# Linear attention, MLP mixer and routed experts on one core: earlier narrowing, second matrices split in order of use, later scalings, a conditional end

## The chip, the core and the metric

The kernel runs on one core of one Trainium2 chip. The metric is the device time of one execution in microseconds (us), from a few runs of the same program; the median is given. Engines are called as the profile's rows call them: PE is TensorE's matmul, PEld its weight load, DVE VectorE, ACT ScalarE, POOL GpSimd, SP SyncE (here only the owner of most DMA queues). A name such as `SPq` is that engine's sequencer or DMA queue.

## The reference

Three stages follow one another on 4 batches of 576 tokens and 512 features. Here the weights of the MLP stage come in as float64, and the kernel narrows them to float32 itself.

```python
# 1: linear attention, 8 heads of 64
proj = q_or_k @ w_phi                                  # 64 -> 128
proj = proj - max(abs(proj), axis=-1)
phi  = concatenate([exp(proj), exp(-proj)], axis=-1)
kv   = einsum('bhsf,bhsd->bhfd', phi_k, v);  z = sum(phi_k, axis=2)
x    = (phi_q @ kv) / (phi_q @ z + 1e-06)
...
# 2: token mixing of rank 32, then a channel MLP 512 -> 2048 -> 512
u = x + (xt @ U @ V).transpose(0, 2, 1)
x = u + maximum(u @ w_ch1, 0.0) @ w_ch2
...
# 3: one expert of 8 for each token (512 -> 1024 -> 512)
fresh_e = argmax(logits[b, s])
e = fresh_e if s == 0 or local_gate[b, s] < 0.5 else prev_e
out[b, s] = p[e] * (maximum(x[b, s] @ w1[e], 0.0) @ w2[e])
```

## The kernel before

**Products.** A matrix product of the two MLP stages is three matmuls in the format that the rows call fp32r: high half by high half, high by low, low by high. So every weight piece (128x512) and every input of a second product exists twice. The high half of a weight is a cast on ACT (L370), its low half a subtraction on DVE (L364); the high half `hhi` of a hidden tile is a relu on ACT (L1106), the low half `hlo` one fused instruction on DVE (L1092). First products are recorded at L1127 to L1129, second ones (`mm2`) at L1249 to L1251. `mm2` goes over four hidden tiles in the order f = 2, 3, 0, 1 and uses the second matrix V2, V3, V0, V1 in that order. Some units save products by sums of submatrices; these sums are DVE instructions recorded at L1090 and L364.

**Narrowing.** Weights of the MLP stage arrive as float64 and are narrowed to float32 by `narrow`: one Abs on ACT (L93) and six instructions on DVE (L97, L100, L102, L104, L107, L111). Raw words sit in two buffers only, `raw0_92` and `raw1_93`. SP refills one (L322) once L107 of the block that used it has read it. During attention the threads `w_first` and `w_park` narrow the 16 pieces of the first two weight units; a narrowed piece is parked in HBM (L403). Attention is a loop of steps `S_`; a step calls `advance("w")` RATE = 2 times in `prepare` and, for each item of MLP work that `ffn_ahead` puts in beside attention from step 24 on, BESIDE = 3 times more if S_ > 21. Each call emits one instruction or a few of the narrowing. Nothing reorders them afterwards: an engine runs its instructions in the order in which the Python code emitted them.

**Banks.** During attention, tiles named `psf`, `tq`, `num`, `tps` and `utps` take turns in the three PSUM banks of the pool `ps_f`: the fourth tile waits until the first has been read out. A `psf` of a first product is read by `hhi` and then `hlo`. `utps` (token mixing, L925) multiplies by `ts`, whose low half is a DVE subtraction (L911).

**MoE.** Eight units, batch b = 0 to 3 and halves g = 0, 1, with 288 columns to a tile. The result of a batch is multiplied by the tokens' probabilities (`scaled`, L1276) and stored (L1285). Such a scaling is due two items after its product; in the last item it follows at once, and its store goes out on SP.

**The end.** Tokens whose expert is none of the two that a batch is served by are handled in a loop over a count `nl`, loaded at L1533 by every engine after all other work. Here the count is 0.

Of the kernel before, what the change touches and what calls it, by code (L numbers as in the profile page):

```python
# [28 lines left out]
NROW = 8  # L29
FT1 = 16  # L30
FT2 = 8
RATE, BESIDE = 2,3
MB = (1,2,3,)

LOCAL_T = -1.5 * 2.0 ** -23
# [6 lines left out]
def model(ctx, tc, kq, vx, wphi, ident, up, vp, wff, wg, wmoe1, wmoe2, rconst, outT):  # L42
    nc = tc.nc
# [10 lines left out]
    ps_f = ctx.enter_context(tc.tile_pool(name="ps_f", bufs=3, space=PSUM))  # L54
# [8 lines left out]
    y = const.tile([128, 4, B * S], F32, name="y")  # L63
# [97 lines left out]
    late = {}  # L161
# [6 lines left out]
    threads = []  # L168
# [11 lines left out]
    def cost(eng, n):  # L180
        return {"DVE": 0.085 + n / 960, "ACT": 0.17 + n / 1330, "POOL": 0.05 + n / 340}[eng]
# [101 lines left out]
    waiting = []  # L283
# [19 lines left out]
        return free_.pop(0)  # L303

    BLOCKS = ("A11", "A12", "A21", "A22")
    VS = ("V0", "V1", "V2", "V3")
    PLAIN = ("A11", "A12", "A21", "A22") + VS
    SEVEN = ("A21", "A11", "A22", "A12") + VS
    order = [(u, n) for u in ffn_units for n in (SEVEN if u.g else PLAIN)]
    wd = dram.tile([2, 8, 128, 512], F32, name="wd")  # L310
    raws = []

    def raw_dma():

# [919 lines left out]
    def mm2(i, t, d):  # L1234
# [296 lines left out]
    nl = nc.values_load(late["left"][0:1, 0:1], min_val=0, max_val=28)  # L1533
    l_p = ctx.enter_context(tc.tile_pool(name="lp", bufs=1))
    with tc.For_i(0, nl):
        f8 = l_p.tile([1, 8], F32, name="l_f8")
        ix = l_p.tile([1, 8], U32, name="l_ix")
        pf = l_p.tile([1, 1], F32, name="l_pf")
        po = l_p.tile([1, 32], F32, name="l_po")
        be = l_p.tile([1, 2], F32, name="l_be")  # L1540
        bi = l_p.tile([1, 3], I32, name="l_bi")
        tmp = l_p.tile([1, 16], F32, name="l_tmp")
        nc.vector.max(out=f8, in_=flags)
        nc.vector.max_index(out=ix, in_max=f8, in_values=flags)
        nc.vector.tensor_copy(out=pf, in_=ix[:, 0:1])
        nc.vector.tensor_scalar(out=po, in0=iota32[0:1], scalar1=pf, scalar2=None, op0=ALU.is_equal)
        nc.vector.tensor_tensor(out=flags, in0=flags, in1=po, op=ALU.subtract)

        nc.vector.tensor_tensor(out=tmp, in0=po[:, 0:16], in1=po[:, 16:32], op=ALU.add)
        nc.vector.tensor_tensor(out=tmp[:, 0:8], in0=tmp[:, 0:8], in1=tmp[:, 8:16], op=ALU.add)  # L1550
        nc.vector.tensor_tensor(out=tmp[:, 0:8], in0=tmp[:, 0:8], in1=iota8[0:1], op=ALU.mult)
        nc.vector.tensor_reduce(out=be[:, 1:2], in_=tmp[:, 0:8], axis=AX, op=ALU.add)
        nc.vector.tensor_tensor(out=be[:, 0:1], in0=pf, in1=be[:, 1:2], op=ALU.subtract)
        nc.vector.tensor_scalar(out=be[:, 0:1], in0=be[:, 0:1], scalar1=0.125, scalar2=None, op0=ALU.mult)

        nc.vector.tensor_copy(out=bi[:, 0:2], in_=be)
        nc.vector.tensor_copy(out=bi[:, 2:3], in_=pf)
        ev = nc.sync.value_load(bi[0:1, 1:2], min_val=0, max_val=NE - 1)
        bs = nc.sync.value_load(bi[0:1, 0:1], min_val=0, max_val=B - 1)
        rs = nc.sync.value_load(bi[0:1, 2:3], min_val=0, max_val=8 * B - 1)  # L1560
        bv = nc.vector.value_load(bi[0:1, 0:1], min_val=0, max_val=B - 1)
        ls = l_p.tile([128, S], F32, name="l_s")
        nc.sync.dma_start(out=ls, in_=late["sall"][bass.ds(rs, 1)].partition_broadcast(128))
        yb = l_p.tile([128, 4, S], F32, name="l_y")
        ob = l_p.tile([128, 4, S], F32, name="l_o")

        nc.sync.dma_start(out=yb, in_=late["ys"][:, :, bass.ds(bs * S, S)])
        nc.vector.memset(ob, 0.0)

        with tc.For_i(0, FT2) as j:  # L1570
            w1, w2 = (l_p.tile([128, 512], F32, name=f"l_w{m}") for m in range(2))
            nc.sync.dma_start(out=w1.rearrange("p (k c) -> p k c", k=2), in_=wmoe1[bass.ds(ev, 1), bass.ds(j, 1)].rearrange("o i k p c -> p (o i k) c"))
            nc.sync.dma_start(out=w2, in_=wmoe2[bass.ds(ev, 1), bass.ds(j, 1)].rearrange("o i p f -> (o i p) f"))
            for c in range(2):
                sl = slice(c * CH, (c + 1) * CH)
                ps = late["psg"].tile([128, CF], F32, tag="f", name="l_ps")[:, :CH]
                for k in range(4):
                    nc.tensor.matmul(ps, lhsT=w1[:, k * 128:(k + 1) * 128], rhs=yb[:, k, sl], start=(k == 0), stop=(k == 3))
                ht = l_p.tile([128, CH], F32, tag="l_h", bufs=2, name="l_h")
                nc.scalar.activation(out=ht, in_=ps, func=ACTF.Relu)  # L1580
                for d in range(4):
                    ps = ps_f.tile([128, CF], F32, tag="f", name="l_acc")[:, :CH]
                    nc.tensor.matmul(ps, lhsT=w2[:, d * 128:(d + 1) * 128], rhs=ht, start=True, stop=True)
                    nc.vector.tensor_tensor(out=ob[:, d, sl], in0=ps, in1=ob[:, d, sl], op=ALU.add)
        nc.vector.tensor_tensor(out=ob, in0=ob, in1=ls.unsqueeze(1).to_broadcast([128, 4, S]), op=ALU.mult)
        dst = y[:, :, bass.ds(bv * S, S)]
        nc.vector.tensor_tensor(out=ob, in0=ob, in1=dst, op=ALU.add)
        nc.vector.tensor_copy(out=dst, in_=ob)
        nc.sync.dma_start(out=outT.rearrange("(k p) t -> p k t", p=128)[:, :, bass.ds(bs * S, S)], in_=ob)
# [78 lines left out]
```

## Time and profile before

| what | value |
|---|---|
| device time, median of 3 runs | 768.52 us |
| the three runs | 767.36, 768.52, 770.09 us |
| device time of the profiled execution | 767.14 us |
| span in its profile, first to last instruction | 765.3 us |
| PE busy | 749.4 us, 98% of the span |
| DVE busy | 614.4 us, 80% |
| ACT busy | 339.0 us, 44% |
| POOL busy | 72.6 us, 9% |
| mean granted TensorE clock | 0.998 of full speed |

The profile is of one execution, and every duration below is from it. The table's share of busy time says which engine is nearest its limit over the whole span; where that engine stands still is seen only by stretches and by waits. The device time holds 1.8 us that lie outside the span.

### The profile page before, as it was taken

What the parts mean: (1) busy time and instruction counts of PE and PEld (TensorE: products, weight loads), DVE (VectorE), ACT (ScalarE), POOL (GpSimd) and SP (SyncE); (2) the same over time, 40 slices, a digit from 0 to 9 for tenths busy, and PEclk for the clock granted to TensorE, in tenths of its full rate; (3) what the DMA queues carried; (4) which work ended last, traced back from release to release, by engine and by line L of the source; (5) the groups of instructions that cost most, each with busy time, mean ns of one, the idle gap of its engine ahead of it and who ended that gap; (6) DMA issues with size and microseconds to landing.
All of it is one profiled execution on the core that took longest, in us unless ns stands there. A gap on an engine that the chain in (4) does not pass through costs nothing.

```text
span 765.3 us, 18800 instructions
## 1 busy us (share of the span) xinstructions
PE 749.4 (98%) x7680; PEld 728.7 (95%) x7680; DVE 614.4 (80%) x1241; ACT 339.0 (44%) x751; POOL 72.6 (9%) x116
## 2 busy tenths in 40 slices
PE   8999999999999999999999999999999999999996
PEld 6899898999899999999999999999999999999996
DVE  7889999887867989896899455256768899999974
ACT  5677767674242533323332222023454457365450
POOL 0212422112200000100101001000000000000000
PEclk9999999999999999999999999999999999999999
DMA  6444746325589687930659007442362143432501
GB/s 204 156 135 152 251 150 215 95 107 207 182 290 375 200 323 270 344 113 2 232 198 312 1 1 256 158 165 84 111 211 98 38 147 110 131 107 81 170 23 63
DMA packets 48344, 123.75 MB, mean 162 GB/s; under 512 B 5440, under 2 KB 20928, under 8 KB 48256
## 3 DMA queue, kind: packets, MB, share of 16 engines
q1 hardware_dynamic: 38640, 86.68, 33.4%
q0 software_dynamic: 6160, 32.39, 12.3%
q10 hardware_dynamic: 3456, 3.46, 1.3%
q8 instruction: 61, 1.00, 0.6%
q14 instruction: 27, 0.22, 0.1%
HBM read 88.55 MB, written 33.96 MB: 160 GB/s over the span
## 4 chain that ended last, share of the span: by engine, by line
PE 79%; DVE 3%; ACT 1%; issue 1%; POOL 0%; ACTq 0%; DVEq 0%
PE psf L1250 13%; PE psf L1249 13%; PE psf L1251 13%; PE psf L1128 12%; PE psf L1127 12%; PE psf L1129 12%; PE kv L848 1%; PE num L882 1%; PE pj L815 1%; PE psf L1297 1%; PE tq L862 0%; DVE row L102 0%; PE tps L908 0%; DVE y L1090 0%; PE utps L925 0%
## 5 line engine op out<-in xcount | busy, mean ns | idle before, releaser
L1250 PE MATMUL psf<-hhi,w 128*128 128x384 f32 (+1 forms) x640 | 203.9, 319 | 1.3 <-DVE w L364 1.3
L1249 PE MATMUL psf<-hhi,w 128*128 128x384 f32 (+1 forms) x640 | 204.4, 319 | 0.0
L1251 PE MATMUL psf<-hlo,w 128*128 128x384 f32 (+1 forms) x640 | 203.6, 318 | 0.0
L1128 PE MATMUL psf<-x,w 128*128 128x384 f32 (+1 forms) x576 | 184.0, 319 | 0.6 <-POOL x L74 0.6
L1127 PE MATMUL psf<-x,w 128*128 128x384 f32 (+1 forms) x576 | 184.3, 320 | 0.0
L1129 PE MATMUL psf<-x,w 128*128 128x384 f32 (+1 forms) x576 | 183.9, 319 | 0.0
L1106 ACT ACTIVATE hhi<-psf 128x384 fp32r<-128x384 f32 (+1 forms) x160 | 69.9, 459 | 129.0 <-DVE psf L1090 98.6
L1250 PEld LDWEIGHTS psf<-hhi,w 128*128 128x128 f32 x640 | 120.1, 188 | 1.7 <-DVE w L364 1.7
L1249 PEld LDWEIGHTS psf<-hhi,w 128*128 128x128 f32 x640 | 120.1, 188 | 1.0 <-issue 0.9
L1251 PEld LDWEIGHTS psf<-hlo,w 128*128 128x128 f32 x640 | 120.1, 188 | 0.0
L1128 PEld LDWEIGHTS psf<-x,w 128*128 128x128 f32 x576 | 108.2, 188 | 1.0 <-POOL x L74 0.9
L1127 PEld LDWEIGHTS psf<-x,w 128*128 128x128 f32 x576 | 108.3, 188 | 0.9 <-DVE hlo L1092 0.5
L1129 PEld LDWEIGHTS psf<-x,w 128*128 128x128 f32 x576 | 108.2, 188 | 0.0
L1090 DVE TENSOR_TENSOR y<-psf,y 128x384 f32<-128x384 f32 (+1 forms) x128 | 67.5, 528 | 47.2 <-PE psf L1251 46.9
L1092 DVE SCALAR_TENSOR_TENSOR hlo<-psf,hhi 128x384 fp32r<-128x384 f32 (+1 forms) x160 | 74.9, 509 | 23.0 <-ACT hhi L1106 22.4
L370 ACT CAST w<-row 128x512 fp32r<-128x512 f32 x75 | 44.5, 619 | 70.1 <-PE psf L1251 30.1
L364 DVE TENSOR_TENSOR w<-row,w 128x512 fp32r<-128x512 f32 x75 | 49.7, 684 | 7.9 <-ACT w L370 7.9
L818 DVE TENSOR_REDUCE mx<-pj 128x6 f32<-128x768 f32 (+2 forms) x49 | 45.7, 934 | 5.5 <-PE pj L815 5.5
L819 DVE TENSOR_TENSOR pg<-pj,mx 128x768 f32<-128x768 f32 (+2 forms) x49 | 46.1, 941 | 2.5
L1090 DVE TENSOR_TENSOR u<-psf,p 128x384 f32<-128x384 f32 (+1 forms) x64 | 32.4, 513 | 19.5 <-PE psf L1129 15.3
L717 POOL DMA_DIRECT2D x<-xd x41 | 21.9, 533 | 270.1 <-PE psf L1129 236.2
L848 PE MATMUL kv<-vt,ek 128*64 128x65 f32 (+1 forms) x1152 | 47.1, 230 | 0.0
(119 smaller groups left out, 990.2 us busy)
## 6 DMA issues: line engine op xcount, KB each, us to landing
x<-xd POOLq DMA_DIRECT2D x41, 768.0 KB, 6.6
raw<-in_wff SPq DMA_DIRECT2D x32, 512.0 KB, 3.9
xd<-x SPq DMA_DIRECT2D x21, 768.0 KB, 6.0
raw<-in_wmoe SPq DMA_DIRECT2D x36, 256.0 KB, 3.4
kq<-in_kq SPq DMA_DIRECT2D x14, 576.0 KB, 4.6
row<-in_wmoe SPq DMA_DIRECT2D x28, 256.0 KB, 3.9
vt<-in_vx SPq DMA_DIRECT2D x16, 325.0 KB, 3.1
ud<-y SPq DMA_DIRECT2D x4, 1152.0 KB, 7.1
```

The lines of the kernel that those rows point to most:

```text
L364: eng.tensor_tensor(out=out, in0=a, in1=b, op=op)
L819: nc.vector.tensor_tensor(out=p[:, :, sl], in0=ps[:, :, sl], in1=mx[:, :, sl].unsqueeze(3).to_broadcast([128, 2, m, 128]), op=ALU.subtract)
L848: nc.tensor.matmul(out[c], lhsT=e[:, half, i, c], rhs=rhs, start=(tl == 0 and half == 0), stop=(tl == 8 and half == 1), skip_group_check=True)
L1090: nc.vector.tensor_tensor(**kw)
L1092: nc.vector.scalar_tensor_tensor(op1=op1, **kw)
L1106: hat[t, f] = act(lambda: nc.scalar.activation(out=hhi, in_=src, func=ACTF.Relu), n_, ready)
L1127: nc.tensor.matmul(ps, lhsT=w[:, 0, c], rhs=x[:, 0, k, :n_], start=(first and k == 0), stop=False, skip_group_check=True)
L1128: nc.tensor.matmul(ps, lhsT=w[:, 0, c], rhs=x[:, 1, k, :n_], start=False, stop=False, skip_group_check=True)
L1129: nc.tensor.matmul(ps, lhsT=w[:, 1, c], rhs=x[:, 0, k, :n_], start=False, stop=(stop and k == 1), skip_group_check=True)
L1249: nc.tensor.matmul(ps, lhsT=wh, rhs=hhi, start=(k == 0), stop=False)
L1250: nc.tensor.matmul(ps, lhsT=wl, rhs=hhi, start=False, stop=False)
L1251: nc.tensor.matmul(ps, lhsT=wh, rhs=hlo, start=False, stop=(k == 3))
```

## The change

Five edits.

1. The number of extra calls of `advance("w")` beside an item goes from 3 at all steps above 21 to a table: 6 at steps 24, 25 and 26, none from 27 on. The blocks are the same, and so is the number of their instructions.
2. The weight planner splits the second matrices in the order V2, V3, V0, V1, in which `mm2` uses them. PIECES keeps the old index for the layout in HBM.
3. A scaling is due four items after its product, not two, and `scale_row` first brings any that are pending for the batch whose buffer it takes.
4. The count of further experts is loaded by all engines just ahead of the last sum of the last product. The loop stands in a conditional block.
5. GpSimd has a drain ahead of that block.

```diff
-RATE, BESIDE = 2,3
+RATE = 2
+BESIDE = {22: 3, 23: 3, 24: 6, 25: 6, 26: 6}
...
-    VS = ("V0", "V1", "V2", "V3")
+    VS = ("V2", "V3", "V0", "V1")
+    PIECES = BLOCKS + tuple(sorted(VS))
...
-            for _ in range(BESIDE if S_ > 21 else 0):
+            for _ in range(BESIDE.get(S_, 0)):
                 advance("w")
...
+        if i + 1 == n and t == 1 and d == 3:
+            late["nl"] = nc.values_load(late["left"][0:1, 0:1], min_val=0, max_val=28)
 
         if u.kind == "moe" and u.g == 0:
             ps_at[m] = act(lambda: nc.scalar.copy(out=dst, in_=ps), n_, at)
...
-                spawn("x", i + 2, scaled(u.b, t, d, t0, dst))
+                spawn("x", i + 4, scaled(u.b, t, d, t0, dst))
...
     def scaled(b, t, d, t0, dst):
 
+        pending[b] = pending.get(b, 0) + 1
+        yield "step"
         yield from gate("DVE", cost("DVE", CH))
         nc.vector.tensor_tensor(out=dst, in0=dst, in1=scale[b][:, t * CH:(t + 1) * CH], op=ALU.mult)
+        pending[b] -= 1
...
     def scale_row(b):
 
+        until(lambda: not pending.get(b - 2), "x")
...
-    nl = nc.values_load(late["left"][0:1, 0:1], min_val=0, max_val=28)
+    nc.gpsimd.drain()
+    nl = late["nl"]
     l_p = ctx.enter_context(tc.tile_pool(name="lp", bufs=1))
-    with tc.For_i(0, nl):
...
+    with tc.If(nl > 0):
+        with tc.For_i(0, nl):
...
```

What the first two edits do to the order of instructions is seen only in the built programs. Line numbers of the changed kernel are one higher up to L300 and two higher from there to L1260. A row is line, operation, written tile, read tiles and size.

ACT in step 24, from the second `hhi` of the item beside attention; `row0_84`, `row2_86` and `row5_89` are blocks being narrowed. Before:

```order
L1106 ACTIVATE hhi_3319<-psf_3306 128x384
L1106 ACTIVATE hhi_3339<-psf_3326 128x384
L93 ACTIVATE row2_86<-raw1_93 128x512
L864 ACTIVATE eq_3351<-tq_3347 128x384
L865 ACTIVATE eq_3351<-tq_3347 128x384
L910 CAST ts_3372<-tps_3366 128x128
L612 CAST x3_105<-y_83 128x768
```

After:

```order
L1108 ACTIVATE hhi_3322<-psf_3309 128x384
L94 ACTIVATE row2_86<-raw1_93 128x512
L1108 ACTIVATE hhi_3346<-psf_3333 128x384
L94 ACTIVATE row5_89<-raw0_92 128x512
L866 ACTIVATE eq_3361<-tq_3357 128x384
L867 ACTIVATE eq_3361<-tq_3357 128x384
L912 CAST ts_3382<-tps_3376 128x128
```

The Abs of block `row2_86` now stands ahead of the third `hhi`, and that of `row5_89`, which stood behind the next item's `hhi` further down, ahead of both exponentials `eq`.

DVE in the same step, from the second `hlo` on to the low half of `ts`. Before:

```order
L1092 SCALAR_TENSOR_TENSOR hlo_3320<-psf_3306,hhi_3319 128x384
L102 SCALAR_TENSOR_TENSOR row0_84<-raw0_92,row0_84 128x512
L104 TENSOR_SCALAR row1_85<-row0_84 128x512
L107 SCALAR_TENSOR_TENSOR row1_85<-raw0_92,row1_85 128x512
L1092 SCALAR_TENSOR_TENSOR hlo_3340<-psf_3326,hhi_3339 128x384
L111 TENSOR_TENSOR row0_84<-row0_84,row1_85 128x512
L911 TENSOR_TENSOR ts_3372<-tps_3366,ts_3372 128x128
```

After:

```order
L1094 SCALAR_TENSOR_TENSOR hlo_3323<-psf_3309,hhi_3322 128x384
L112 TENSOR_TENSOR row0_84<-row0_84,row1_85 128x512
L98 TENSOR_SCALAR row3_87<-row2_86 128x512
L101 TENSOR_SCALAR row2_86<-row3_87 128x512
L103 SCALAR_TENSOR_TENSOR row2_86<-raw1_93,row2_86 128x512
L1094 SCALAR_TENSOR_TENSOR hlo_3347<-psf_3333,hhi_3346 128x384
L105 TENSOR_SCALAR row3_87<-row2_86 128x512
L108 SCALAR_TENSOR_TENSOR row3_87<-raw1_93,row3_87 128x512
L112 TENSOR_TENSOR row2_86<-row2_86,row3_87 128x512
L98 TENSOR_SCALAR row4_88<-row5_89 128x512
L913 TENSOR_TENSOR ts_3382<-tps_3376,ts_3382 128x128
```

Three instructions of block `row2_86` now stand between the second and the third `hlo`, and its other three and the first one of `row5_89` ahead of `ts`.

DVE in step 25, from the `hlo` of that step's item to its `ts`. Before:

```order
L1092 SCALAR_TENSOR_TENSOR hlo_3461<-psf_3447,hhi_3460 128x384
L102 SCALAR_TENSOR_TENSOR row2_86<-raw1_93,row2_86 128x512
L104 TENSOR_SCALAR row3_87<-row2_86 128x512
L107 SCALAR_TENSOR_TENSOR row3_87<-raw1_93,row3_87 128x512
L1090 TENSOR_TENSOR y_83<-psf_3467,y_83 128x384
L111 TENSOR_TENSOR row2_86<-row2_86,row3_87 128x512
L911 TENSOR_TENSOR ts_3498<-tps_3492,ts_3498 128x128
```

After:

```order
L1094 SCALAR_TENSOR_TENSOR hlo_3471<-psf_3457,hhi_3470 128x384
L105 TENSOR_SCALAR row4_88<-row5_89 128x512
L108 SCALAR_TENSOR_TENSOR row4_88<-raw0_92,row4_88 128x512
L112 TENSOR_TENSOR row5_89<-row5_89,row4_88 128x512
L98 TENSOR_SCALAR row6_90<-row7_91 128x512
L1092 TENSOR_TENSOR y_83<-psf_3481,y_83 128x384
L101 TENSOR_SCALAR row7_91<-row6_90 128x512
L103 SCALAR_TENSOR_TENSOR row7_91<-raw1_93,row7_91 128x512
L105 TENSOR_SCALAR row6_90<-row7_91 128x512
L108 SCALAR_TENSOR_TENSOR row6_90<-raw1_93,row6_90 128x512
L112 TENSOR_TENSOR row7_91<-row7_91,row6_90 128x512
L913 TENSOR_TENSOR ts_3515<-tps_3509,ts_3515 128x128
```

Ahead of `ts` stand now the rest of block `row5_89` and DVE's whole share of block `row7_91`, ten instructions where there were five.

DVE in the MoE item in which batch 2 begins, from the first `hlo` on; `w3_97` and `w8_3732` are low halves of two of the second matrices. Before:

```order
L1092 SCALAR_TENSOR_TENSOR hlo_8478<-psf_8461,hhi_8477 128x288
L1092 SCALAR_TENSOR_TENSOR hlo_8482<-psf_8468,hhi_8481 128x288
L1092 SCALAR_TENSOR_TENSOR hlo_8500<-psf_8375,hhi_8499 128x288
L1092 SCALAR_TENSOR_TENSOR hlo_8503<-psf_8382,hhi_8502 128x288
L1092 SCALAR_TENSOR_TENSOR hlo_8454<-psf_8399,hhi_8453 128x288
L1092 SCALAR_TENSOR_TENSOR hlo_8459<-psf_8406,hhi_8458 128x288
L1090 TENSOR_TENSOR psf_8420<-psf_8420,u20_3751 128x288
L1090 TENSOR_TENSOR psf_8427<-psf_8427,u21_3752 128x288
L364 TENSOR_TENSOR w3_97<-row4_88,w3_97 128x512
L364 TENSOR_TENSOR w8_3732<-raw0_92,w8_3732 128x512
L1276 TENSOR_TENSOR y_83<-y_83,scale1_3756 128x288
```

After:

```order
L1094 SCALAR_TENSOR_TENSOR hlo_8472<-psf_8456,hhi_8471 128x288
L1094 SCALAR_TENSOR_TENSOR hlo_8476<-psf_8463,hhi_8475 128x288
L1094 SCALAR_TENSOR_TENSOR hlo_8493<-psf_8373,hhi_8492 128x288
L1094 SCALAR_TENSOR_TENSOR hlo_8496<-psf_8380,hhi_8495 128x288
L1094 SCALAR_TENSOR_TENSOR hlo_8449<-psf_8396,hhi_8448 128x288
L1094 SCALAR_TENSOR_TENSOR hlo_8454<-psf_8403,hhi_8453 128x288
L1092 TENSOR_TENSOR psf_8415<-psf_8415,u20_3751 128x288
L1092 TENSOR_TENSOR psf_8422<-psf_8422,u21_3752 128x288
L366 TENSOR_TENSOR w8_3732<-row0_84,w8_3732 128x512
```

The low half in `w3_97` is now split ahead of these rows, together with two others; that in `w8_3732` stays behind the two sums of `psf`, and no scaling is left in this place.

## Rows read from the trace of the kernel before

**Rows 1.** Busy time of each engine in three stretches (instructions in brackets), clock, DMA share.

```profile
165.00:210.00 45.00, 43.43 (x489) 41.22 (x486) 35.83 (x73) 19.26 (x42) 10.15 (x10) 1.00 0.52 175
220.00:660.00 440.00, 440.00 (x2763) 436.18 (x2762) 341.85 (x719) 155.04 (x318) 25.86 (x49) 1.00 0.49 169
660.00:680.00 20.00, 18.66 (x140) 18.27 (x140) 19.56 (x43) 10.53 (x24) 0.00 (x0) 1.00 0.49 156
```

**Rows 2.** What TensorE waited for over the whole span.

```profile
PE psf L1250 <- DVE w L364: 1.3, 1, 1.3
PE utps L925 <- DVE ts L911: 0.9, 1, 0.9
```

**Rows 3.** SyncE's timeline, 171 to 172 us: start, length, what is issued.

```profile
171.31 0.33 SPq L322 DMA_DIRECT2D raw<-in_wff  x1
```

**Rows 4.** The page's DMA issues: KB each, median us to landing.

```profile
raw<-in_wff SPq DMA_DIRECT2D x32, 512.0 KB, 3.9
```

**Rows 5.** ScalarE's timeline, 163 to 212 us.

```profile
175.11 0.49 ACT L1106 ACTIVATE hhi<-psf 128x384 fp32r<-128x384 f32 x1 [1.59 <-PE psf L1129]
175.71 0.70 ACT L93 ACTIVATE row<-raw 128x512 f32<-128x512 f32 x1
...
188.99 0.67 ACT L93 ACTIVATE row<-raw 128x512 f32<-128x512 f32 x1 [0.79 <-DMA raw<-in_wff]
```

**Rows 6.** VectorE's timeline, 163 to 212 us.

```profile
174.03 0.68 DVE L102 SCALAR_TENSOR_TENSOR row<-raw,row 128x512 uint32<-128x512 uint32 x1
174.75 0.43 DVE L104 TENSOR_SCALAR row<-row 128x512 uint32<-128x512 uint32 x1
175.21 0.69 DVE L107 SCALAR_TENSOR_TENSOR row<-raw,row 128x512 f32<-128x512 uint32 x1
175.82 0.55 DVE L1092 SCALAR_TENSOR_TENSOR hlo<-psf,hhi 128x384 fp32r<-128x384 f32 x1
176.28 0.68 DVE L111 TENSOR_TENSOR row<-row,row 128x512 f32<-128x512 f32 x1
...
183.17 0.56 DVE L1092 SCALAR_TENSOR_TENSOR hlo<-psf,hhi 128x384 fp32r<-128x384 f32 x1 [1.56 <-ACT hhi L1106]
...
186.65 0.29 DVE L911 TENSOR_TENSOR ts<-tps,ts 128x128 fp32r<-128x128 f32 x1
...
188.75 1.13 DVE L100 TENSOR_SCALAR row<-row 128x512 uint32<-128x512 uint32 x1
```

**Rows 7.** TensorE's timeline, 171 to 206 us.

```profile
176.53 0.27 PE L882 MATMUL num<-kvs,eq 128*64 128x65 f32 x1
...
187.31 0.48 PE L925 MATMUL utps<-vs,ts 128*128 128x256 f32 x2
```

**Rows 8.** GpSimd's timeline, 163 to 212 us.

```profile
187.42 2.17 POOL L74 TENSOR_TENSOR x<-y,x 128x384 fp32r<-128x384 f32 x2 [7.33 <-ACT x L612]
```

**Rows 9.** The chain that ended last, 669 to 675 us.

```profile
671.56 1.18 DVE hlo L1092 x3
...
673.02 0.45 DVE psf L1090
673.48 0.60 DVE w L364
```

**Rows 10.** TensorE's timeline, 672.2 to 674.6 us.

```profile
672.37 0.30 PE L1129 MATMUL psf<-x,w 128*128 128x288 f32 x1
672.50 0.29 PE L1249 MATMUL psf<-hhi,w 128*128 128x288 f32 x1
```

**Rows 11.** The scalings' line: duration minimum, median, maximum in ns; first and last start.

```profile
L1276 DVE TENSOR_TENSOR y<-y,scale x24: 435/450/455, 608.5 to 723.0; 128x288 f32<-128x288 f32 x24
```

**Rows 12.** VectorE's timeline, 754 to 766 us.

```profile
758.78 0.46 DVE L1090 TENSOR_TENSOR y<-y,scale 128x288 f32<-128x288 f32 x1
```

**Rows 13.** DMA issues, 740 to 766 us.

```profile
outT<-y SPq DMA_DIRECT2D x8, 144.0 KB, 1.7
```

**Rows 14.** Instructions of the program's closing line, ns minimum, median, maximum.

```profile
L1663 POOLq DRAIN  x3: 40/107/2352, 762.1 to 765.0; - x3
```

More of the change, by code (lines that the diff above doesn't have):

```diff
@@ L316, in raw_dma @@
             u, name = order.pop(0)
-            i = (BLOCKS + VS).index(name)
+            i = PIECES.index(name)
             t = rawfree.pop(0)
@@ L402, in park @@
     def park(u, s, f):
-        nc.sync.dma_start(out=wd[u.g, (BLOCKS + VS).index(s)], in_=f[:, :512])
+        nc.sync.dma_start(out=wd[u.g, PIECES.index(s)], in_=f[:, :512])
     def w_park():
@@ L438, in parked @@
                 yield "wait"
-            nc.sync.dma_start(out=f[:, :512], in_=wd[u.g, (BLOCKS + VS).index(name)])
+            nc.sync.dma_start(out=f[:, :512], in_=wd[u.g, PIECES.index(name)])
             emitted[0] += 1
@@ L1273, in scaled @@
     def scaled(b, t, d, t0, dst):
+        pending[b] = pending.get(b, 0) + 1
+        yield "step"
         yield from gate("DVE", cost("DVE", CH))
         nc.vector.tensor_tensor(out=dst, in0=dst, in1=scale[b][:, t * CH:(t + 1) * CH], op=ALU.mult)
+        pending[b] -= 1
         outs.append((outT[d * 128:(d + 1) * 128, t0:t0 + CH], dst))
     outs = []
+    pending = {}
     def store(keep):
@@ L1527, in model @@
         pass
-    assert not routes and not waiting
+    assert not routes and not waiting and not threads
     right.close()
-    nl = nc.values_load(late["left"][0:1, 0:1], min_val=0, max_val=28)
+    nc.gpsimd.drain()
+    nl = late["nl"]
     l_p = ctx.enter_context(tc.tile_pool(name="lp", bufs=1))
-    with tc.For_i(0, nl):
[L1536 to L1589, printed above, removed]
@@ new lines, in model @@
+    with tc.If(nl > 0):
+        with tc.For_i(0, nl):
+            f8 = l_p.tile([1, 8], F32, name="l_f8")
+            ix = l_p.tile([1, 8], U32, name="l_ix")
+            pf = l_p.tile([1, 1], F32, name="l_pf")
+            po = l_p.tile([1, 32], F32, name="l_po")
+            be = l_p.tile([1, 2], F32, name="l_be")
+            bi = l_p.tile([1, 3], I32, name="l_bi")
+            tmp = l_p.tile([1, 16], F32, name="l_tmp")
+            nc.vector.max(out=f8, in_=flags)
+            nc.vector.max_index(out=ix, in_max=f8, in_values=flags)
+            nc.vector.tensor_copy(out=pf, in_=ix[:, 0:1])
+            nc.vector.tensor_scalar(out=po, in0=iota32[0:1], scalar1=pf, scalar2=None, op0=ALU.is_equal)
+            nc.vector.tensor_tensor(out=flags, in0=flags, in1=po, op=ALU.subtract)
+            nc.vector.tensor_tensor(out=tmp, in0=po[:, 0:16], in1=po[:, 16:32], op=ALU.add)
+            nc.vector.tensor_tensor(out=tmp[:, 0:8], in0=tmp[:, 0:8], in1=tmp[:, 8:16], op=ALU.add)
+            nc.vector.tensor_tensor(out=tmp[:, 0:8], in0=tmp[:, 0:8], in1=iota8[0:1], op=ALU.mult)
+            nc.vector.tensor_reduce(out=be[:, 1:2], in_=tmp[:, 0:8], axis=AX, op=ALU.add)
+            nc.vector.tensor_tensor(out=be[:, 0:1], in0=pf, in1=be[:, 1:2], op=ALU.subtract)
+            nc.vector.tensor_scalar(out=be[:, 0:1], in0=be[:, 0:1], scalar1=0.125, scalar2=None, op0=ALU.mult)
+            nc.vector.tensor_copy(out=bi[:, 0:2], in_=be)
+            nc.vector.tensor_copy(out=bi[:, 2:3], in_=pf)
+            ev = nc.sync.value_load(bi[0:1, 1:2], min_val=0, max_val=NE - 1)
+            bs = nc.sync.value_load(bi[0:1, 0:1], min_val=0, max_val=B - 1)
+            rs = nc.sync.value_load(bi[0:1, 2:3], min_val=0, max_val=8 * B - 1)
+            bv = nc.vector.value_load(bi[0:1, 0:1], min_val=0, max_val=B - 1)
+            ls = l_p.tile([128, S], F32, name="l_s")
+            nc.sync.dma_start(out=ls, in_=late["sall"][bass.ds(rs, 1)].partition_broadcast(128))
+            yb = l_p.tile([128, 4, S], F32, name="l_y")
+            ob = l_p.tile([128, 4, S], F32, name="l_o")
+            nc.sync.dma_start(out=yb, in_=late["ys"][:, :, bass.ds(bs * S, S)])
+            nc.vector.memset(ob, 0.0)
+            with tc.For_i(0, FT2) as j:
+                w1, w2 = (l_p.tile([128, 512], F32, name=f"l_w{m}") for m in range(2))
+                nc.sync.dma_start(out=w1.rearrange("p (k c) -> p k c", k=2), in_=wmoe1[bass.ds(ev, 1), bass.ds(j, 1)].rearrange("o i k p c -> p (o i k) c"))
+                nc.sync.dma_start(out=w2, in_=wmoe2[bass.ds(ev, 1), bass.ds(j, 1)].rearrange("o i p f -> (o i p) f"))
+                for c in range(2):
+                    sl = slice(c * CH, (c + 1) * CH)
+                    ps = late["psg"].tile([128, CF], F32, tag="f", name="l_ps")[:, :CH]
+                    for k in range(4):
+                        nc.tensor.matmul(ps, lhsT=w1[:, k * 128:(k + 1) * 128], rhs=yb[:, k, sl], start=(k == 0), stop=(k == 3))
+                    ht = l_p.tile([128, CH], F32, tag="l_h", bufs=2, name="l_h")
+                    nc.scalar.activation(out=ht, in_=ps, func=ACTF.Relu)
+                    for d in range(4):
+                        ps = ps_f.tile([128, CF], F32, tag="f", name="l_acc")[:, :CH]
+                        nc.tensor.matmul(ps, lhsT=w2[:, d * 128:(d + 1) * 128], rhs=ht, start=True, stop=True)
+                        nc.vector.tensor_tensor(out=ob[:, d, sl], in0=ps, in1=ob[:, d, sl], op=ALU.add)
+            nc.vector.tensor_tensor(out=ob, in0=ob, in1=ls.unsqueeze(1).to_broadcast([128, 4, S]), op=ALU.mult)
+            dst = y[:, :, bass.ds(bv * S, S)]
+            nc.vector.tensor_tensor(out=ob, in0=ob, in1=dst, op=ALU.add)
+            nc.vector.tensor_copy(out=dst, in_=ob)
+            nc.sync.dma_start(out=outT.rearrange("(k p) t -> p k t", p=128)[:, :, bass.ds(bs * S, S)], in_=ob)
```

## The prediction

> **What bounds the kernel now.** I read the busy time by stretches first. From 220 to 660 us PE is busy 440.00 of 440.00 us at the full clock [rows 1]. There only fewer or faster matmuls would help, and the change touches none. PE stands still in the attention stretch (43.43 of 45.00 us from 165 to 210), in a 20-us stretch of the MoE stage (18.66) [rows 1], and behind its last matmul. PE's waits name the two largest stalls after the start: 1.3 us for a low half of a weight (L364) and 0.9 us for the low half of `ts` (L911) [rows 2]. In both DVE is late. The end comes last: VectorE's last product starts at 758.78 and takes 0.46 us [rows 12], but drains of the closing line start as late as 765.0, and one of GpSimd's takes 2.352 us [rows 14]. These three places are what the change can reach; everything else is hidden behind PE unless it makes PE wait anew.
>
> **Narrowing sooner, the gain.** The 0.9 us wait [rows 2] comes late in attention, where narrowing instructions stand ahead of `ts`. With BESIDE none from step 27 on, the orders show none between the last item's sums and `ts`. What stays is the chain from the last matmul into `tps` over ACT's cast to `ts`, which I put at 0.1 us beyond the matmuls that cover it. Gain 0.8 us.
>
> **Narrowing sooner, the cost in step 24.** There are two raw buffers. The refill for block `row2_86` was issued at 171.31 [rows 3], the median refill lands 3.9 us later [rows 4], and its Abs ran at 175.71, for 0.70 us [rows 5]. Nothing ahead of that refill is moved, so the Abs can't start sooner than before. Now it stands ahead of the third `hhi`, which had run at 175.11 [rows 5]. DVE can begin this block at about 176.4, and needs L97, L100 and L102 ahead of the third `hlo`. L102 took 0.68 us, L104 0.43, L107 0.69 [rows 6]; L97 and L100 I take at L104's 0.43, as they are of the same operation. With the gaps between them that is 1.6 us. So `hlo` starts at 178.0 and ends at 178.5 (its 0.55 us is in the same rows), where it had started at 175.82. `num` takes the bank that this `hlo` sets free, and had started at 176.53, right behind it [rows 7]. It now starts at about 178.6: PE loses 2.1 us.
>
> **The cost in step 25.** All of PE is 2.1 us later. The `hlo` that began at 183.17 [rows 6] begins at 185.25. Between its start and `ts` stood 3.48 us (186.65 less 183.17 [rows 6]), five instructions besides itself. Now there are ten besides itself; the added ones are five narrowing instructions, three of 0.43 and two of 0.69 [rows 6] (L111 taken as L107), together 2.7 us, with gaps 2.9. So `ts` starts at 185.25 + 3.5 + 2.9 = 191.65 and ends 0.29 later, at 191.95. PE's first `utps` matmul at L925 stood ready at 187.31 [rows 7], now at 189.4: 2.5 us more. The Abs of that block is not what is late: its refill goes out behind L107 of `row2_86`, at about 179.7, and lands by 183.6, ahead of the relu of 184.7. While PE waits nothing behind it can catch up, so both stalls add: 4.6 us.
>
> One price is open. L100 at 188.75 took 1.13 us [rows 6] where its neighbours of that operation took 0.43, while GpSimd ran two subtractions from 187.42 on for 2.17 us [rows 8]. In the changed kernel the same pair falls at about 189.5 to 191.7, into the ten instructions. Two of them could take 0.7 us more, so the bounds of this cost are 0 and 1.4; in the row that I have one of DVE's instructions was hit in full and one in part, but sums with a PSUM input stand there too. I take 0.4.
>
> The Trainium skill, SBUF — State Buffer, section "SBUF: two separate sides", says that the pair of ports that VectorE and GpSimd share is an exclusive lock and that the loser waits for the whole instruction. The row of 1.13 us agrees: it ends 0.3 us behind GpSimd's pair. By that rule the full 1.4 would be lost and the sum below would be 1.0 us higher.
>
> For this edit then 4.6 + 0.4 - 0.8 = +4.2 us. Bounds: -0.9, if the refills and DVE's gaps cover all of it (the wait of [rows 2] alone goes), and +5.4 with the port in full and a refill 0.2 us late. Cover would have to come from idle time of DVE: 45.00 - 35.83 = 9.2 us in this stretch [rows 1], but it lies behind waits for PE such as the 1.56 us ahead of the `hlo` at 183.17 [rows 6], and a wait for a landing cannot be moved forward: at 188.99 the Abs waited 0.79 us for one even at the old pace [rows 5].
>
> **Order of the second matrices.** The wait of 1.3 us [rows 2] follows the matmul at 672.50 [rows 10]. The chain up to it is three `hlo` from 671.56 (1.18 us), a sum at 673.02 (0.45) and the split of V2's low half at 673.48, 0.60 us long [rows 9]. After the change three of the four low halves are ready ahead; the one left is that of V1, the last that `mm2` uses. It still stands behind the two sums and ends at about 674.1. PE wants it ten matmuls after 672.50. Over 440 us a matmul took 440.00/2763 = 0.16 us [rows 1], with the wider tiles of the MLP stage in it; at that ten take 1.6 us, so PE wants it by 674.1 or, as these tiles are narrow, sooner. Of the stall 0 to 0.3 us stays, so the gain is 1.1 us. Below nothing cannot be excluded elsewhere, since the planner emits in another order in all units; bounds 0 and 1.4.
>
> **Scalings later.** 24 instructions of 0.45 us [rows 11], none added; they leave DVE where it is tight (19.56 of 20.00 us busy [rows 1]). Their stores move with them and none is among the last. What hides them is PE's own work; without that cover one scaling costs 0.45 us. Taken as 0, bounds -0.4 and +0.9 (two that meet a sum that PE waits for).
>
> **The end.** The count is loaded ahead of the last sum on DVE. No row prices the load; the nearest is one DVE instruction there, 0.46 us [rows 12], so its bounds are 0 and 0.5. I take 0.1, since DVE waits ahead of that sum for PE's last matmul anyhow. Taking it off the end saves little: SP's wait for the last store covers it. The last store goes out when DVE ends at 759.24 [rows 12] and lands 1.7 us after issue [rows 13], near 761 to 762. GpSimd's drain of 2.352 us starts at 762.1 [rows 14], once the waits for the last transfers are over, so it lies wholly behind the landing. In the changed program GpSimd has nothing to wait for at the end: the final waits stand on SP alone, the loop is passed over by a branch, and GpSimd, which had no busy instruction from 660 to 680 already [rows 1], drains early. If the 2.35 us are a cost of GpSimd's first drain after its work, they are then hidden behind PE. Gain 2.3 us, bounds 0 and 2.4.
>
> **Sum.** +4.2 - 1.1 + 0 + 0.1 - 2.3 = +0.9 us. The profiled execution took 767.14 us, which is 1.4 below the median of 768.52; against its own time 768.0, as a median about 769.4. From no change a measurement of this kernel tells about 0.3%, that is 2.3 us.
>
> **Rivals.**
> First, the earlier narrowing is hidden: DVE's 9.2 us of idle time take it up, `num` and `utps` start as before. For it: seven blocks are the same work, and the stretch is not full. Against it: the two orders above, in which work that PE waits for stands behind a landing. Then -0.9 - 1.1 - 2.2 = -4.2: 764.3 us. It decides once the edit costs less than 1.0 us net, that is once the two stalls and the port together stay under 1.8 us.
>
> Second, on the other side, the end keeps its drain: it is a cost of the closing line wherever the core's last transfers end, not of GpSimd's first. For it: the row names the closing line, and three drains of 40 to 2352 ns follow one another there [rows 14]. Against it: only GpSimd's is long. Then +4.2 - 1.1 + 0.1 = +3.2: 771.7 us. It decides when more than 1.4 us of the 2.35 stays, as 0.9 + 1.4 is the 2.3 of a measurable loss.
>
> Third, the stalls of step 24 and 25 are longer: each block behind is late by the one ahead of it, as two buffers go round. With the port's 1.4 and one more late refill of 0.8 us (the wait at 188.99 [rows 5]) the edit costs 6.0: 771.2 us. It decides once the edit costs over 5.6.
>
> The rule of the SBUF page of the Trainium skill, cited above, speaks for the first half of this rival and gives it no more than its 1.4 us; by the lock alone, with the refills on time, the time would be 770.4, still within a measurement of no change.
>
> **How the numbers follow.** My forecast, no change within 0.3%, has 0.55, of which its edges give 0.01 to faster and 0.02 to slower; the first rival 0.22; the second 0.12, of which a third still falls within 0.3%, since an edit 1 somewhat cheaper brings it back; the third 0.09; what I have not seen 0.02 to slower. That gives faster 0.23, same 0.56, slower 0.21. The forecast's own range is 767.4 to 770.8. For 8 in 10 it must reach to the first rival's gentler half and to the second and third: 764.8 to 771.9.
>
> **What would show it.** Right: PE waits of about 2 us each at `num` (L884) and `utps` (L927) between 176 and 193 us, released by DVE; the wait for `ts` near 204 us gone; at 672 us a stall of 0.3 instead of 1.3; GpSimd's long drain far ahead of the end and the span ending some 3.7 us behind the last product instead of 6 (765.3, the span, less 759.24). Wrong: no new wait between 170 and 195 us (then 764), a drain still behind the landing (then near 772), or a new wait for L366 or a sum in the MoE stage.

## The result: slower by half a per cent

The changed kernel took 772.58 us (median of 5 runs, 770.80 to 773.59), the kernel before 768.06 us on the same occasion (5 runs): a ratio of 1.0054, interval 1.0040 to 1.0067. The forecast was 769.4 us with a range of 764.8 to 771.9, and no change the likeliest. The time lies above the range. The profiled execution spans 768.9 us, against 765.3.

PE's waits of the changed kernel, over the whole span:

```profile
PE utps L927 <- DVE ts L913: 3.2, 1, 3.2
...
PE num L884 <- DVE hlo L1094: 1.4, 1, 1.4
PE num L884 <- ACT eq L867: 1.1, 2, 0.9
...
PE psf L1252 <- DVE w L366: 0.2, 1, 0.2
```

The two waits of [rows 2] are gone or small: the one for a low half of a weight is 0.2 us now, and the 0.9 us wait for `ts` near 204 us is not the 3.2 us listed here, which is that of step 25. The waits at `num` are those of step 24, where the prediction put them. Waits alone don't give the result: 3.2 + 1.4 + 0.9 (the longest of the two at `eq`) are 5.5 us new, 0.9 + 1.1 gone, and the end won more than 2, so they leave some 1 us of the 3.6 between the two spans. The rest is in the clock. The same trace by stretches of 2 us, with columns as in [rows 1] (the third figure from the end, ahead of DMA share and GB/s, is the granted clock):

```profile
188.00:190.00 2.00, 2.00 (x46) 1.93 (x45) 1.95 (x5) 1.42 (x3) 0.00 (x0) 1.00 0.85 201
190.00:192.00 2.00, 0.27 (x3) 0.07 (x1) 1.92 (x3) 0.67 (x1) 1.98 (x2) 1.00 0.50 193
192.00:194.00 2.00, 0.50 (x2) 0.51 (x3) 1.93 (x5) 0.01 (x1) 0.69 (x1) 0.59 0.54 180
194.00:196.00 2.00, 2.00 (x8) 2.00 (x7) 1.90 (x5) 1.06 (x2) 0.00 (x0) 0.50 0.94 376
196.00:198.00 2.00, 2.00 (x8) 2.00 (x7) 0.90 (x3) 0.00 (x0) 0.00 (x0) 0.50 0.62 243
198.00:200.00 2.00, 2.00 (x10) 2.00 (x10) 1.93 (x5) 0.00 (x0) 0.00 (x0) 0.71 0.73 257
200.00:202.00 2.00, 2.00 (x13) 2.00 (x12) 1.91 (x4) 0.00 (x0) 0.00 (x0) 1.00 0.35 132
```

PE stands still from 190.3 to 193.5 us. Its granted clock falls while it stands (0.59 in the stretch from 192 on) and is 0.50, the lower level of 1.2 GHz, until some time after 198 us. From 193.5 on PE is busy all that while and gets less done: 8 matmuls in 2 us, where 13 stand from 200 on. PE's timeline shows it matmul by matmul:

```profile
189.91 0.36 PE L927 MATMUL utps<-vs,ts 128*128 128x256 f32 x1
193.50 0.58 PE L927 MATMUL utps<-vs,ts 128*128 128x256 f32 x1 [3.23 <-DVE ts L913]
193.87 0.53 PE L1251 MATMUL psf<-hhi,w 128*128 128x384 f32 x1
194.20 0.52 PE L1252 MATMUL psf<-hhi,w 128*128 128x384 f32 x1
...
199.25 0.33 PE L1253 MATMUL psf<-hlo,w 128*128 128x384 f32 x1
199.43 0.34 PE L1251 MATMUL psf<-hhi,w 128*128 128x384 f32 x1
```

From 193.87 on one matmul starts 0.32 to 0.33 us behind the other, from 199.25 on 0.18. The 17 matmuls between take 199.25 - 193.87 = 5.4 us; at 0.18 they would take 3.0. These 2.4 us stand in no list of waits, since PE waited for nothing.

What made the two stalls is to be seen on ACT and DVE. ACT in step 24:

```profile
175.22 0.70 ACT L94 ACTIVATE row<-raw 128x512 f32<-128x512 f32 x1 [1.82 <-DMA raw<-in_wff]
175.82 0.48 ACT L1108 ACTIVATE hhi<-psf 128x384 fp32r<-128x384 f32 x1
179.65 0.67 ACT L94 ACTIVATE row<-raw 128x512 f32<-128x512 f32 x1 [3.35 <-DMA raw<-in_wff]
180.23 0.47 ACT L866 ACTIVATE eq<-tq 128x384 f32<-128x384 f32 x1
```

The Abs at 175.22 waited 1.82 us for its raw words with the third `hhi` behind it. That of 179.65 waited 3.35 us with both `eq` exponentials behind it (the second `num` needs them). DVE in steps 24 and 25:

```profile
177.55 0.55 DVE L1094 SCALAR_TENSOR_TENSOR hlo<-psf,hhi 128x384 fp32r<-128x384 f32 x1
...
185.76 0.56 DVE L1094 SCALAR_TENSOR_TENSOR hlo<-psf,hhi 128x384 fp32r<-128x384 f32 x1 [0.73 <-ACT hhi L1108]
...
190.01 0.43 DVE L105 TENSOR_SCALAR row<-row 128x512 uint32<-128x512 uint32 x1
190.48 1.36 DVE L108 SCALAR_TENSOR_TENSOR row<-raw,row 128x512 f32<-128x512 uint32 x1
191.87 1.37 DVE L112 TENSOR_TENSOR row<-row,row 128x512 f32<-128x512 f32 x1
193.16 0.28 DVE L913 TENSOR_TENSOR ts<-tps,ts 128x128 fp32r<-128x128 f32 x1
```

The third `hlo` starts at 177.55 (175.82 before, [rows 6]), `ts` of step 25 at 193.16 (186.65 before). Ahead of it two narrowing instructions took 1.36 and 1.37 us. GpSimd ran its pair of subtractions just then:

```profile
190.02 2.67 POOL L75 TENSOR_TENSOR x<-y,x 128x384 fp32r<-128x384 f32 x2 [5.99 <-ACT x L614]
```

The end, by VectorE's last product, the new drain and the closing line:

```profile
765.09 0.46 DVE L1092 TENSOR_TENSOR y<-y,scale 128x288 f32<-128x288 f32 x1
```

```profile
L1542 POOLq DRAIN  x1: 2347/2347/2347, 719.5 to 719.5; - x1
```

```profile
L1674 POOLq DRAIN  x3: 34/107/122, 722.4 to 768.7; - x3
```

GpSimd's 2.347 us now start at 719.5, and the closing drains take 0.034 to 0.122 us. From the start of the last product to the end of the span it is 768.9 - 765.09 = 3.8 us, against 765.3 - 758.78 = 6.5 before [rows 12].

### The profile page after: what moved, and what is told of

Its sections match the earlier page's. It is cut to its first block, busy times and chain, and to the rows that moved or that the text cites. A ratio compares the mean times of both kernels' runs of the same rounds, so it can differ in the third digit from the quotient of the medians.

```text
span 768.9 us, 18731 instructions
## 1 busy us (share of the span) xinstructions
PE 752.1 (98%) x7680; PEld 731.0 (95%) x7680; DVE 615.3 (80%) x1241; ACT 338.5 (44%) x751; POOL 72.5 (9%) x116
## 6 DMA issues: line engine op xcount, KB each, us to landing
x<-xd POOLq DMA_DIRECT2D x41, 768.0 KB, 6.6
xd<-x SPq DMA_DIRECT2D x21, 768.0 KB, 5.7
```

## The experiments

The theory after the result: edit 1 carries all of the loss, by two stalls and, with the second, a fall of TensorE's clock; edits 2 to 5 win nearly 4 us. They ran in four groups (e1 to e4, e5 to e8, e9 and e10, e11 and e12), each group on one chip beside the kernel before (768.0 to 768.1 us on each occasion).

**e1, edit 1 alone.**

```diff
-RATE, BESIDE = 2,3
+RATE = 2
+BESIDE = {22: 3, 23: 3, 24: 6, 25: 6, 26: 6}
...
-            for _ in range(BESIDE if S_ > 21 else 0):
+            for _ in range(BESIDE.get(S_, 0)):
```

> The kernel before with the table of extra calls alone. Theory (the narrowing moved sooner carries the whole loss, and costs more than its waits, since the granted clock falls behind the second one): TensorE 7.7 us later by the end of attention, as in the changed kernel's trace, and nothing won elsewhere: 7.0 to 8.4 us over the kernel before, granted clock 0.5 for some 5 us near 195 us. Rival (the loss of the changed kernel is made by its edits together, the narrowing alone costs the 4.2 us that the prediction gave it): 3.5 to 5 us over before, clock at 1.00 throughout.

Measured: 775.45 us, before 768.11; ratio 1.0088, interval 1.0066 to 1.0110. PE's longest waits from 165 us on and the stretches with the fall of the clock:

```profile
PE utps L926 <- DVE ts L912: 3.2, 1, 3.2
PE num L883 <- DVE hlo L1093: 1.8, 1, 1.8
PE psf L1251 <- DVE w L365: 1.3, 1, 1.3
PE num L883 <- ACT eq L866: 0.7, 1, 0.7
```

```profile
192.00:194.00 2.00, 0.14 (x1) 0.14 (x1) 1.93 (x5) 0.25 (x1) 1.06 (x1) 0.72 0.34 106
194.00:196.00 2.00, 2.00 (x7) 2.00 (x8) 1.90 (x5) 0.70 (x2) 0.00 (x0) 0.50 0.96 382
196.00:198.00 2.00, 2.00 (x8) 2.00 (x7) 1.19 (x3) 0.35 (x1) 0.00 (x0) 0.50 0.74 298
```

The theory holds: 7.3 us, the same stalls, the same half clock, and the wait of 1.3 us of the MoE stage still there.

**e2, edits 2 to 5 alone.** Against the changed kernel:

```diff
-BESIDE = {22: 3, 23: 3, 24: 6, 25: 6, 26: 6}
+BESIDE = {k: 3 for k in range(22, 40)}
```

> The changed kernel with the old rule of three extra calls at every step above 21, so edits 2 to 5 alone. Theory: attention as before, the wait of 1.3 us at 672 us gone, GpSimd's drain of 2.35 us hidden: 3.5 to 4.5 us under the kernel before. Rival (the end and the order of the second matrices win only part, the new order makes waits of its own in the last 100 us): 0 to 2 us under before.

Measured: 764.39 us, before 768.11; ratio 0.9946, interval 0.9927 to 0.9965: 3.7 us won, within what the theory gave, and outside the rival's. So the change is a gain of 3.7 us and a loss of 7.3, together +3.6; measured were +4.5, with an interval of 3.1 to 5.1 (0.40% to 0.67%).

**e3, the wait filled.** The changed kernel, with the wait for `ts` in step 25 filled by matmuls that add zero.

```diff
...
         for n2 in range(2):
             nc.tensor.matmul(ps[:, :n_], lhsT=t[:, n2], rhs=vs[:, s0:s0 + n_], start=False, stop=(n2 == 1), skip_group_check=True)
+            if n2 == 0 and (g, half) == FILL:
+                for _ in range(27):
+                    nc.tensor.matmul(ps[:, :n_], lhsT=zr, rhs=vs[:, :n_], start=False, stop=False, skip_group_check=True)
```

> The changed kernel with 27 matmuls of a zero tile put between the two L927 matmuls of step 25, adding zero to the same bank; they take about 3.2 us and fit into the 3.2 us wait for ts. Nothing else is changed. Theory (the half rate from 193 to 199 us is the clock, which falls because TensorE stood still): granted clock 1.00 there, the matmuls behind the wait 0.175 us apart, not 0.32, and about 2.6 us under the changed kernel, 1.0 to 2.3 over before. Rival (the half rate comes of contention for memory with the narrowing and the transfers of that stretch): still 0.32 us apart and within 0.5 us of the changed kernel.

Measured: 769.70 us, before 768.11; ratio 1.0024, interval 1.0013 to 1.0035. That is 2.9 us under the changed kernel, by the medians of two occasions on which the kernel before took 768.06 and 768.11. The size is rough, as the five runs of the changed kernel are spread over 2.8 us, but the intervals of the two ratios don't meet. The two profiled executions are 1.3 us apart (spans of 768.9 and 767.6), with longer waits at `num` in that of e3 (1.7 and 1.2 us, not 1.4 and 0.9). PE's timeline, with the fillers as one row, and the stretches:

```profile
190.97 3.37 PE L933 MATMUL utps<-vs,zr 128*128 128x256 f32 x27
194.41 0.39 PE L930 MATMUL utps<-vs,ts 128*128 128x256 f32 x1
194.63 0.34 PE L1257 MATMUL psf<-hhi,w 128*128 128x384 f32 x1
194.81 0.34 PE L1258 MATMUL psf<-hhi,w 128*128 128x384 f32 x1
194.98 0.34 PE L1259 MATMUL psf<-hlo,w 128*128 128x384 f32 x1
```

```profile
190.00:194.00 4.00, 4.00 (x50) 3.93 (x47) 3.86 (x5) 1.49 (x3) 2.72 (x2) 1.00 0.49 160
194.00:200.00 6.00, 5.93 (x35) 5.72 (x35) 5.73 (x15) 1.05 (x2) 0.00 (x0) 1.00 0.84 311
```

`ts` comes no sooner (the matmul that needs it starts at 194.41), and behind it DVE and the transfers are busier than in the changed kernel from 194 to 200 us (5.73 us and a DMA share of 0.84, against 4.72 and 0.76), yet the clock is 1.00 and matmuls start 0.17 to 0.18 us apart. So the half rate was the clock's and not contention, and it came of PE's standing still. PE did 3.4 us of useless work and the kernel was 2.9 us faster by the medians.

**e4, GpSimd's pair out of the way.**

```diff
-            for _ in range(2):
+            for _ in range({25: 1, 26: 3}.get(S_, 2)):
                 advance("x")
```

> The changed kernel with one call of the input thread moved from step 25 to step 26, so that GpSimd's two subtractions (L75) leave the stretch in which VectorE runs the ten instructions ahead of ts. Theory (the two instructions of 1.36 and 1.37 us were held by GpSimd): they take 0.69 us, ts comes 1.3 us sooner, the wait for ts is 1.9 instead of 3.2 us; 1.3 us under the changed kernel, and 2.6 more if the clock then doesn't fall. Rival (VectorE's instructions are long there for another reason): wait for ts 3.0 us or more, time as the changed kernel.

Measured: 769.19 us, before 768.11; ratio 1.0011, interval 0.9998 to 1.0023: 3.4 us under the changed kernel. DVE's last instructions ahead of `ts`, PE's two longest waits from 165 us on, and the stretches around step 24:

```profile
192.59 0.69 DVE L108 SCALAR_TENSOR_TENSOR row<-raw,row 128x512 f32<-128x512 uint32 x1
193.32 0.69 DVE L112 TENSOR_TENSOR row<-row,row 128x512 f32<-128x512 f32 x1
193.93 0.28 DVE L913 TENSOR_TENSOR ts<-tps,ts 128x128 fp32r<-128x128 f32 x1
```

```profile
PE num L884 <- DVE hlo L1094: 2.3, 1, 2.3
PE utps L927 <- DVE ts L913: 1.9, 1, 1.9
```

```profile
178.00:180.00 2.00, 0.19 (x6) 0.20 (x8) 1.93 (x5) 0.00 (x0) 0.00 (x0) 1.00 0.74 283
180.00:182.00 2.00, 2.00 (x44) 2.00 (x43) 1.83 (x4) 1.24 (x3) 0.00 (x0) 0.53 0.35 107
182.00:184.00 2.00, 2.00 (x42) 2.00 (x41) 0.96 (x4) 1.45 (x4) 0.84 (x1) 0.62 0.92 275
```

The two instructions take 0.69 us each, and the wait is 1.9 us, both as the theory had them. The clock doesn't fall behind it. It does fall in this trace at step 24, where a wait of 2.3 us in one piece stands in place of the 1.4 and 0.9 of the changed kernel's trace; what it costs there takes in part the place of the wait for `eq`, which is gone from the list. Up to there the engines run the same instructions in both traces. What differs is the landing: the Abs ahead of the third `hhi` waited 2.78 us for its raw words in this trace, not 1.82. So whether the clock fell at step 24 varied with the execution, and the later landing is the likely cause, not one that was tested.

**e5, e6 and e7, the end.** e5 is the kernel before with edits 4 and 5. e6 is e2 without the drain. e7 is the kernel before with the drain and nothing else:

```diff
+    nc.gpsimd.drain()
     nl = nc.values_load(late["left"][0:1, 0:1], min_val=0, max_val=28)
```

> The kernel before with edits 4 and 5 alone (count loaded ahead of the last sum, loop in a conditional block, early drain). Theory (GpSimd's drain of 2.35 us leaves the path): span ends some 3.6 us behind VectorE's last product instead of 6.0; 2.2 to 2.6 us under before, the wait of 1.3 us at 672 us stays. Rival (the end gives only what the earlier load of the count saves, and the rest of the gain of edits 2 to 5 comes from the MoE stage): 0.3 to 1.0 us under before.

> Edits 2 to 4 without the early drain of edit 5 (and without edit 1). Theory (the long drain is a cost of GpSimd's first drain after its last work, wherever it stands; in the conditional program GpSimd waits for nothing and comes to its closing drains early): the closing line's first drain takes 2.35 us near 720 us, the time is that of edits 2 to 5, 3.3 to 4.2 us under before. Rival (the explicit drain is what moves it): the 2.35 us are back behind the last store, 1.0 to 1.8 us under before.

> The kernel before with one GpSimd drain ahead of the load of the count, and nothing else. Theory (first drain after the last work is the long one, a later one is short): 2.35 us at the new line near 712 us, the closing drains 0.1 us each, 2.2 to 2.5 us under before. Rival (a drain in the closing line is long because GpSimd then has waits or a branch behind it, the conditional block is what takes it away): both are long, time as before within 0.4 us.

Measured, with 768.13 for before: e5 765.84 us (ratio 0.9968, interval 0.9959 to 0.9977), e6 763.95 (0.9955, 0.9939 to 0.9970), e7 766.38 (0.9976, 0.9966 to 0.9985). GpSimd's drains of the closing line in e6, of the new line in e7, and of the closing line in e7:

```profile
L1673 POOLq DRAIN  x3: 34/107/2427, 712.2 to 761.2; - x3
```

```profile
L1533 POOLq DRAIN  x1: 3032/3032/3032, 624.6 to 624.6; - x1
```

```profile
L1664 POOLq DRAIN  x3: 40/46/107, 763.0 to 763.8; - x3
```

The long drain is GpSimd's first behind its work, wherever it stands: in e6, with no explicit drain, a closing one of 2.427 us comes as early as 712, in e7 the explicit one takes 3.032 us at 624.6 and the closing ones are short. Either edit 4 or the drain of edit 5 takes it off the path; with edit 4 in place the drain of edit 5 buys nothing that shows (763.95 without, 764.39 with, on different occasions). e7 misses its 2.2 to 2.5 us by a little (1.75), and e5's 2.3 are within its own; the half microsecond between them would be what edit 4 has beyond the drain, but their intervals overlap.

**e9 and e10, the MoE stage.** Edit 2 alone and edit 3 alone, as in the diff of the change.

> The kernel before with edit 2 alone (second matrices split in the order V2, V3, V0, V1). In its order two low halves still stand behind the sums of psf in the item at 672 us, those of V0 and V1 now. Theory (edit 2 needs edit 3, which lets the third low half go ahead; alone it only moves the wait from V2's matmul to V0's, seven matmuls later): the wait of 1.3 us falls to about 0.6 us, 0.5 to 0.9 us under before. Rival (as the prediction put it, edit 2 alone takes the wait away and edit 3 is worth nothing): the wait is 0.3 us or less, 1.1 to 1.5 us under before.

> The kernel before with edit 3 alone (scalings due four items later). In its order three low halves stand ahead of the sums and only the fourth, V3's, behind them. Theory (both edits are needed): V3 is wanted four matmuls after the wait of before began, so a wait of 0.9 to 1.0 us stays, 0.3 to 0.6 us under before. Rival (edit 3 is worth nothing): wait of 1.3 us and the time as before; or (edit 3 carries all): wait 0.3 us, 1.1 to 1.5 us under before.

Measured, with 768.04 for before: e9 767.31 us (ratio 0.9991, interval 0.9982 to 1.0000), e10 767.43 (0.9994, 0.9985 to 1.0003). The times alone hardly tell the two from no change; what is left of the wait of 1.3 us does. e9, then e10:

```profile
PE psf L1251 <- DVE w L365: 0.5, 1, 0.5
```

```profile
PE psf L1250 <- DVE w L364: 0.9, 1, 0.9
```

0.5 and 0.9 us are left, against 0.2 with both edits. In e10's order the scalings are out of the way and the third low half goes ahead of the sums; in e9's it does not. By these waits, of one profile each, either edit does a part, and edit 3 was not worth nothing.

**e8, e11 and e12, a better version.** e8 has edits 2 to 5, and two narrowing instructions moved behind `ts` in step 27, by leaving out the calls of `advance("w")` at one item. Against the changed kernel:

```diff
-            for _ in range(BESIDE.get(S_, 0)):
+            for _ in range(0 if ahead[0] == 15 else BESIDE.get(S_, 0)):
...
-BESIDE = {22: 3, 23: 3, 24: 6, 25: 6, 26: 6}
+BESIDE = {k: 3 for k in range(22, 28)} | {28: 6}
```

> Edits 2 to 5, with three extra calls at each item as in the kernel before, save that the last item of step 27 has none and the one of step 28 six: the two narrowing instructions that stood ahead of ts there come behind it, nothing else ahead of step 27 moves. Theory (the wait of 0.9 us near 204 us is these two instructions): the wait falls to 0.1 or 0.2 us, 0.8 us under edits 2 to 5 alone, 4.2 to 5.0 under before. Rival (what is taken off ts comes back behind it, at the next sum and its bank): same time as edits 2 to 5 alone, 3.7 under before, with a new wait of TensorE between 205 and 212 us.

> The kernel of e8 (edits 2 to 5, two narrowing instructions moved behind ts in step 27), beside that of e2 on one chip. Theory (the 0.9 us wait for ts is won and not given back): 0.6 to 0.9 us under the other run of this call. Rival (given back behind ts, or below what a run can tell): within 0.3 us of it.

> The kernel of e2 (edits 2 to 5 alone) again, as the other half of the pair: 3.4 to 4.0 us under the kernel before by both theories.

Measured: e8 763.79 us, before 768.13; ratio 0.9947, interval 0.9931 to 0.9962. As that is too near to e2, which ran on another occasion, both ran again on one chip: e11, the kernel of e8, 763.25 us (ratio 0.9934, interval 0.9920 to 0.9948), e12 764.50 (0.9948, 0.9934 to 0.9962), before 768.05. The wait for `ts` in e12; e11's list has none:

```profile
PE utps L927 <- DVE ts L913: 0.9, 1, 0.9
```

e11 is 1.25 us under e12, more than the 0.6 to 0.9 expected. This wait explains 0.9; the rest is too small for five runs of each (762.87 to 763.49 and 763.52 to 764.72) and stays open. What edit 1 was after, taking narrowing off `ts`, was to be had by moving two instructions back.

## Why the prediction was wrong

**The step that failed** is the price of step 25's stall. The prediction found the place, its cause and nearly its length, and counted the wait alone: "2.5 us more", "both stalls add: 4.6 us". It took for granted that PE goes on at the same rate behind a wait. Behind this one it ran at half its clock for some 5.5 us, 2.4 us more (the trace above), and e3, which fills the wait and leaves `ts` as late as it was, won 2.9 us by the medians. A rival with this in it was missing. The Trainium skill, TensorE: Matmul & The Clock Gate, Part 1, says that the throttled clock is the default and that activity releases it. The rows agree: full clock ahead of the stall, 0.50 behind it, and 1.00 throughout once e3 kept PE at work. The rows of the kernel before showed no such price, with a clock of 1.00 in all stretches [rows 1]; in its trace the clock falls only at the end (0.84 from 760 to 764 us), when PE has no work left.

**The second miss** is the port, taken at 0.4 us of its bounds of 0 and 1.4. It cost 1.3, near the upper bound: 1.36 + 1.37 against 0.69 each in e4. Both were instructions that started while GpSimd's pair ran (190.02, for 2.67 us), other ones than that of [rows 6]; L105, which started 0.01 us ahead of the pair, took its usual 0.43. The rule of the Trainium skill, SBUF — State Buffer, section "SBUF: two separate sides", which the prediction cites, is that of an exclusive lock. The trace agrees with it in size: by that rule the prediction had the full 1.4 us lost.

**Term by term**, in us: step 24, +2.1 forecast, 1.4 + 0.9 = 2.3 in the waits. That the sum nearly fits is in part luck. The first Abs started at 175.22, sooner than the prediction held possible (175.71 before, when it stood behind a relu and not behind its landing, [rows 5]), so the stall at the third `hlo` was shorter; the 0.9 is the second `num` behind `eq`, behind an Abs that waited for its landing, which the prediction overlooked. Step 25 without the port, +2.5, and 1.9 by e4's wait. Port, +0.4, and 1.3. Clock, nothing, and 2.4 by the trace. Late wait for `ts`, -0.8, and -0.9: the waits of the changed kernel list none there. Edit 1 in all: +4.2 forecast, +7.3 in e1; the terms measured here add up to 7.0. MoE stage, -1.1, and 0.2 of 1.3 left in the trace; the size was right, but it was put down to edit 2 alone with edit 3 at 0, and e9 and e10 show that both have a part. The end, -2.2 net, and -2.3 in e5. Edits 2 to 5 in all: -3.3 forecast, -3.7 in e2.

**The rivals.** The first (hidden narrowing) is refuted by the waits and by e1. The second (the end keeps its drain) is refuted by the closing drains of the changed kernel, 0.034 to 0.122 us, and by e5 to e7. The third (longer stalls by the port and late refills) had the right sign and, at 771.2 us, nearly the time, but its cause is only in part what happened: the port in full, yes; the other part was the clock.

**Left open.** Why the clock fell behind 3.2 us of waiting in the changed kernel and e1, behind 2.3 us at step 24 in e4, and not behind e4's 1.9 us of step 25, is not settled by one profile of each; the other executions have no trace that shows where their clock fell. Nor was it tried whether a third raw buffer would take the refill out of ACT's way.

## What to carry to other kernels

A stall of TensorE can cost more than its length, by what the clock takes behind it (3.2 us and 2.4 more here); price both, and look at the granted clock behind a stall, since the list of waits doesn't hold this. In an in-order queue an instruction that waits for a transfer is as dear as what stands behind it: before moving work sooner, read when its input lands and what it is moved ahead of. Where a bundle comes out near nothing, undo its parts one by one; here a loss of 7 us hid a gain of 4.

## What was not expected of the hardware

Matmuls that add zero kept the clock at 1.00 through a wait of 3.4 us, and made the kernel 2.9 us faster, by the medians, than standing still. GpSimd's first drain after its last work took 2.35 to 3.03 us: 3.032 in e7, where it stands right behind the last transfers that GpSimd issued (624.6), and still 2.347 in the changed kernel, where the last of these was issued at 631.66 and the drain started at 719.5. Later ones took 0.034 to 0.122.
